# Rotation tables from one scaled base, fold by halves, value sums chosen per period, last exps by query halves and 103 VectorE bursts in a fused state-space and attention kernel

## The chip, the cores and the metric

The kernel runs on one core of a Trainium2 chip. The metric is the device time of one execution in microseconds (us). Most executions of a kernel agree within 0.3%. Engines: PE is TensorE (matmul), PEld its weight loads, DVE is VectorE, ACT is ScalarE, POOL is GpSimd, SP is SyncE.

## The reference, cut to what matters

```python
def reference(A_x, A_Lambda_re, ..., B_x, B_wqkv, B_wo, gate_w):      # cut
    x = A_x                                     # 1 x 2048 x 1024, bf16
    g = _sigmoid((x * gate_w).sum(-1, keepdims=True))
    # A: diagonal complex state space, 1024 states
    Lam_bar = jnp.exp(dt * Lam)
    B_bar = ((Lam_bar - 1.0) / Lam)[:, None] * Bmat
    # h[t] = Lam_bar * h[t-1] + B_bar x[t];   a = 2 Re(C h) + x * Dskip
    # B: attention with 32 heads of 32 channels, softmax over 2048 keys
    p = _softmax(q @ k.T * (Dh ** -0.5)); b = (p @ v) @ wo
    return g * a + (1 - g) * b
```

Two things matter for the argument. The attention needs 32 x 2048 x 2048 exponentials, which is what ScalarE does for nearly the whole time (busy for 904.4 of 920.3 us). The state space is done with "rotation tables" (sines and cosines of multiples of each state's angle, built on VectorE), scans on VectorE, and dense matmuls before and after them.

## The kernel before

The exps are 512 *bursts* of two tiles of 128x1024. Around each burst lies a *period*: PE does the scores of the next burst, some quarters of value sums (exps times V, four 33-column matmuls each) and up to five *dense* 512-column matmuls of projections and state space. Dense matmuls gather in one output bank, which VectorE must *evict* before PE can start the next group (the prediction shows such a wait, 0.40 us at 292.82). In some bursts ("VectorE bursts") ScalarE does half of the first tile less, and four VectorE instructions do it instead.

The order of instructions on every engine is fixed when the kernel is built. A layout program in it carries a clock for PE, ScalarE and VectorE, made of figures written into it, and fills VectorE's gaps by them. The gaps of the first 16 bursts, the *opening*, are filled by `spare`:

```python
    def spare(self, us):
        while self.nmath and us > 0:
            us -= self.bg2[0][0]            # booked cost of the next small instruction
            self.nmath -= 1
            self.bg2.pop(0)[1]()
    # ... in the opening, behind an eviction of Q: self.spare(0.5); of V: self.spare(1.0)

    def fill(self, limit):                  # behind the opening
        while True:
            for src in self.sources():
                c = src[0][0]               # booked cost
                # ... cut
                if c == 0 or self.dve_t + c <= limit:
                    src.pop(0)[1]()
                    self.dve_t += c
                    # ... cut
```

The tables, eight blocks of two products and two sums, with their booked costs:

```python
    def table_ops(self, j):
        # ... lo, lor, hi: two short series, broadcast to 128 x 2 x 32 x 16
        for k, y in ((0, lo), (2, lor)):
            ops.append((1.136, lambda ...: e.tensor_tensor(prod[:, k:k + 2], hi, y, ALU.mult)))
        for r, op in ((0, ALU.subtract), (1, ALU.add)):
            ops.append((0.6, lambda ...: e.tensor_tensor(out, prod[:, 2 * r], prod[:, 2 * r + 1], op)))
```

How many quarters of value sums a period gets is a cap, and the dense matmuls have a quota:

```python
            cap = 5
            if p in DVB or p + 1 in DVB:            # DVB: the VectorE bursts
                cap = 3
            # ... n = min(cap, ready), 6 in a few places
            quota = 3 if p in DVB else 5 if p + 1 in DVB and ... else MM_PER_PERIOD
```

The end, cut: sums of burst 510, four preloading matmuls, sums of 511, one reciprocal, two norms, transposition, checks and flag while PE transposes, outputs, evictions.

```python
        self.pv([(NBURST - 2, q) for q in range(4)])
        preload()
        self.pv([(NBURST - 1, q) for q in range(4)])
        # reciprocal, norm and transposition of both query tiles
        check(63, 64, 63, 65, 2)
        # flag; outputs; evictions; stores
```

## Time and profile before

| | before |
|---|---|
| median of 3 runs | 921.74 us (921.31 to 922.07) |
| span of the profiled run | 920.3 us |
| busy: ScalarE, PE, VectorE | 904.4, 884.9 (from an incomplete record, see the result), 758.0 us |
| start of burst 0; start of burst 72 | 9.82; 142.56 us |
| bursts 72 to 504 (93 VectorE bursts among them) | 754.56 us |
| burst 504 to the end of the last exp | 14.40 us |
| last exp to the end of the span | 8.79 us |

The lines are shown in the prediction. How to read such a kernel: when one engine is busy nearly all the time, "busy" says little. The starts of its 1024 instructions say more. What a burst takes from its start to the next one's above 2 x 0.904 us (or 0.478 + 0.904 for a VectorE burst; the prediction works out these steps) is its *lateness*.

### The profile page before, as it was taken

The numbers are of one execution on the slowest core, as the hardware profiler recorded it, in microseconds if no ns is written. First come the engines' busy times: TensorE is split into PE (matmuls) and PEld (weight loads), VectorE is DVE, ScalarE is ACT, GpSimd is POOL, SyncE is SP. The second block draws the span as 40 slices with busy tenths as digits, with TensorE's granted clock in tenths as the row PEclk, the third lists the DMA queues.
The fourth block names the chain that finished last, engine by engine and source line by source line (L and its number), as shares of the span: only waits on it lengthen the run. The fifth ranks groups of instructions, "written<-read, shape, count | busy, mean of one in ns | idle before, by whom it ended". The sixth has DMA issues, their size and how long they took to land.

```text
span 920.3 us, 33392 instructions
## 1 busy us (share of the span) xinstructions
PE 884.9 (96%) x14969; PEld 516.3 (56%) x15188; DVE 758.0 (82%) x1369; ACT 904.4 (98%) x1034; POOL 6.5 (1%) x31
## 2 busy tenths in 40 slices
PE   8999999999999999999999999999999999999996
PEld 4556655755575555565557555556655655555553
DVE  2799999999989889999889975669999866675665
ACT  6999999999999999999999999999999999999996
POOL 0000000000000000000000000000000000000000
PEclk9999999999999999999999999999999999999998
DMA  9546822213302324112142113123320212524312
GB/s 200 111 82 114 120 48 40 47 42 73 82 9 56 62 59 93 47 36 53 51 82 43 42 46 86 44 63 53 51 64 8 68 60 82 162 78 131 113 63 75
DMA packets 166436, 65.35 MB, mean 71 GB/s; under 512 B 146704, under 2 KB 154896, under 8 KB 166288
## 3 DMA queue, kind: packets, MB, share of 16 engines
q1 hardware_dynamic: 164128, 62.62, 30.6%
q8 instruction: 120, 1.97, 0.9%
q10 hardware_dynamic: 2160, 0.53, 0.3%
q14 instruction: 28, 0.23, 0.1%
HBM read 21.24 MB, written 12.58 MB: 37 GB/s over the span
## 4 chain that ended last, share of the span: by engine, by line
ACT 69%; PE 25%; DVE 2%; SPq 1%; issue 1%; DMA 1%; DVEq 0%
ACT f_pt L1693 59%; PE f_ps L1765 7%; PE f_ps L1677 5%; PE f_ps L1513 4%; PE f_ps L1485 4%; PE f_ps L1453 3%; ACT f_wb L1716 2%; ACT f_OT L1693 2%; ACT f_Et L1693 2%; ACT f_cT_re L1693 2%; ACT f_cT_im L1693 2%; PE f_ps L1473 1%; ACT f_ub L1716 1%; SPq L1080 1%; DMA f_xT<-in_A_x_dram 1%
## 5 line engine op out<-in xcount | busy, mean ns | idle before, releaser
L1693 ACT ACTIVATE f_pt<-f_ps 128x1024 bf16<-128x1024 f32 x848 | 801.8, 1141 | 1.2 <-PE f_ps L1677 1.0
L1765 PEld LDWEIGHTS f_ps<-f_V,f_pt 128*128 128x128 bf16 x6784 | 235.0, 96 | 136.5 <-issue 86.6
L1765 PE MATMUL f_ps<-f_V,f_pt 128*128 128x33 bf16 x6784 | 288.4, 178 | 0.3
L1677 PE MATMUL f_ps<-f_Q,f_K 32*128 32x256 bf16 x4096 | 217.9, 273 | 6.8 <-ACT f_cT_re L1693 1.0
L1677 PEld LDWEIGHTS f_ps<-f_Q,f_K 32*128 32x128 bf16 x4096 | 70.3, 92 | 122.6 <-ACT f_pt L1693 62.3
L1485 PE MATMUL f_ps<-f_xT,f_wb 128*128 128x512 bf16 x449 | 117.5, 377 | 7.2 <-issue 2.4
L1453 PE MATMUL f_ps<-f_xT,f_wb 128*128 128x512 bf16 x406 | 106.6, 378 | 5.0 <-issue 1.0
L1399 DVE TENSOR_TENSOR_SCAN f_ht<-f_pf,f_init,f_ut 128x512 bf16<-128x512 f32 x64 | 81.0, 1274 | 0.0
L1717 DVE TENSOR_SCALAR f_wb<-f_ps 128x512 f32<-128x512 f32 x77 | 52.8, 686 | 27.7 <-PE f_ps L1677 27.2
L1513 PE MATMUL f_ps<-f_cT_im,f_hp 128*128 128x512 bf16 x183 | 69.1, 378 | 3.0 <-DVE f_Ag L1522 0.5
L1540 PE MATMUL f_ps<-f_wb,f_OT 128*128 128x512 bf16 x219 | 58.0, 378 | 2.1 <-DVE f_xT L1546 0.2
L1473 PE MATMUL f_ps<-f_wb,f_xT 128*128 128x128 bf16 x896 | 59.1, 219 | 0.0
L1485 PEld LDWEIGHTS f_ps<-f_xT,f_wb 128*128 128x128 bf16 x512 | 40.2, 96 | 33.4 <-issue 1.2
L1513 PE MATMUL f_ps<-f_cT_re,f_hp 128*128 128x512 bf16 x153 | 57.8, 378 | 0.6
L1716 ACT ACTIVATE f_wb<-f_ps 128x512 bf16<-128x512 f32 x77 | 53.8, 699 | 0.0
L1724 DVE SCALAR_TENSOR_TENSOR f_wb<-f_Ag,f_wb 128x512 int16<-128x512 f32 x77 | 52.7, 684 | 0.7
L1723 DVE SCALAR_TENSOR_TENSOR f_Ag<-f_wb,f_Ag 128x512 f32<-128x512 uint16 x77 | 52.7, 685 | 0.6
L1722 DVE SCALAR_TENSOR_TENSOR f_Ag<-f_wb 128x512 f32<-128x512 uint16 x77 | 52.6, 683 | 0.1
L1453 PEld LDWEIGHTS f_ps<-f_xT,f_wb 128*128 128x128 bf16 x464 | 36.2, 96 | 28.7 <-issue 0.4
L1473 PEld LDWEIGHTS f_ps<-f_wb,f_xT 128*128 128x128 bf16 x896 | 50.5, 97 | 0.2
L1546 DVE SCALAR_TENSOR_TENSOR f_xT<-f_ps,f_gcol,f_hp 128x512 bf16<-128x512 f32 (+1 forms) x28 | 21.0, 751 | 26.6 <-PE f_ps L1540 26.6
L1391 DVE TENSOR_TENSOR f_tq<-f_ht,f_Et 128x1024 bf16<-128x1024 bf16 x64 | 42.5, 685 | 0.3
(143 smaller groups left out, 872.1 us busy)
## 6 DMA issues: line engine op xcount, KB each, us to landing
ag_scratch<-f_Ag SPq DMA_DIRECT2D x32, 256.0 KB, 2.0
f_hp<-ag_scratch SPq DMA_DIRECT2D x32, 256.0 KB, 2.8
f_wb<-in_B_wqkv_dram SPq DMA_DIRECT2D x21, 256.0 KB, 4.1
out_dram<-f_xT SPq DMA_DIRECT2D x16, 256.0 KB, 2.0
f_xa<-in_A_x_dram SPq DMA_DIRECT2D x32, 64.0 KB, 2.0
f_pf<-in_A_x_dram SPq DMA_DIRECT2D x32, 64.0 KB, 2.0
f_wb<-in_B_wo_dram SPq DMA_DIRECT2D x1, 1024.0 KB
f_OT<-f_On SPq DMA_TRANSPOSE x63, 2.3
```

The costliest lines, as they stand in the source:

```text
L1399: ops.append((1.192, lambda ri=ri: dve(lambda e: e.tensor_tensor_scan(ht[:, ri, :], rr, ut[:, ri, :], self.init[:, ri, j:j + 1], ALU.mult, ...
L1453: mms.append((1, lambda e, f, l, a=a: e.matmul(ps[:, bank, :], w[:, g % 2, part, a, :], xT[:, a, 512 * ch:512 * (ch + 1)], start=f, stop=l ...
L1473: m = e.matmul(ps[:, bank, 128 * q:128 * (q + 1)], xT[:, a, 128 * kt:128 * (kt + 1)], w[:, g % 2, 2, a, :], start=(a == 0), stop=(a == 7))
L1485: mms.append((1, lambda e, f, l, a=a: e.matmul(ps[:, 7, :], bT[:, n % 2, ri, a, :], xT[:, a, 512 * ch:512 * (ch + 1)], start=f, stop=l), [ ...
L1513: mms.append((1, lambda e, f, l, j=j, ri=ri: e.matmul(ps[:, 7, :], hp(tq, ri, j), cT[ri][:, j, 512 * cb:512 * (cb + 1)], start=f, stop=l), ...
L1540: mms.append((1, lambda e, f, l, j=j: e.matmul(ps[:, 7, :], OT[:, j, 256 * qb + 128 * r:256 * qb + 128 * (r + 1)], wo[j][0][:, 512 * cb:51 ...
L1677: m = e.matmul(ps[:, 2 * sl[z] + h % 2, 256 * kl:256 * (kl + 1)], K[32 * h:32 * h + 32, g % 2, 128 * kt:128 * (kt + 1)], Q[32 * h:32 * h + ...
L1693: self.act(lambda e: e.activation(self.tile[p], ps[:, 2 * s:2 * s + 2, :], ACT.Exp, bias=OCTAVES * LN2, scale=LN2 / 128), [("S", s)], [("p ...
L1716: self.S.op("act", lambda e: e.activation(t[:, 0, :], ps[:, 2 * s, :], ACT.Exp, bias=OCTAVES * LN2, scale=LN2 / 128), reads=[("S", s)], wr ...
L1717: self.S.op("dve", lambda e: e.tensor_scalar(xi, ps[:, 2 * s + 1, :], BITS_0, BITS_MIN, ALU.add, ALU.max), reads=[("S", s)], writes=[("xi" ...
L1723: (0.603, lambda: self.dve(lambda e: e.scalar_tensor_tensor(xw, lo, CUBE_C, xw, ALU.add, ALU.mult), [I, W], [W], "exp_c")),
L1765: m = e.matmul(ps[:, 6, o:o + 33], self.tile[p][:, h2, 256 * kl + 128 * qt:256 * kl + 128 * (qt + 1)], V[:, g % 2, 2 * i + kl, h, :], star ...
```

## The change

Its intent: free VectorE of table and series work, use that for 7 more VectorE bursts (96 to 103), fit the value sums to what is left of each period, and shorten the end by working on query halves. The diff, cut to its core:

```diff
-DVB_RUNS = ((65, 65), (70, 70), ... (508, 508))           # 96 bursts
+DVB_RUNS = ((67, 67), (70, 70), ... (506, 510))           # 103 bursts; ORDER of dense groups is new as well
+PV_FREE = 72
+SPARE_K = (0.0, 0.0, 0.7, 1.3, 1.3, 2.2, 1.0, 0.8)        # gaps filled behind K's evictions, too
+SPARE_V = (1.0, 0.7, 1.3, 1.3, 1.3, 1.3, 1.3, 1.3)
+PV_MOST = 7
+PV_ROUND = 0.5
@@ series: 232 columns rather than 400; then the base, among the opening's small instructions
+        for n, (u, v) in enumerate(((0, 0), (1, 1), (0, 1), (1, 0))):
+            add(1.14, lambda e, ...: e.tensor_tensor(pr[n]..., hi[u], lo[v], ALU.mult), ...)
+        for r, op in ((0, ALU.subtract), (1, ALU.add)):
+            add(1.14, lambda e, ...: e.tensor_tensor(self.base[:, r], pr[2 * r], pr[2 * r + 1], op), ...)
@@ tables: per block of eight one copy, three scalings, six sums
+            ops.append((0.21, lambda: self.dve(lambda e: e.tensor_scalar(sc(a), base, w(1, a), None, ALU.mult), ...
+            ops.append((0.21, lambda: self.dve(lambda e: e.scalar_tensor_tensor(out(r, a), base[:, r], w(0, a), sc(a)[:, 1 - r], ALU.mult, op), ...
@@ fold: 512 columns at a time, booked 0.35 and 0.62, and begun as each block of C lands
@@ 24 two-column copies from VectorE to GpSimd
@@ value sums from burst 72 on
+        n = int((ta - self.T - QK_PE - dense * MM_PE - 0.1) / PV_PE + PV_ROUND)
+        n = max(min(n, PV_MOST), least, 1)
@@ from burst 508 on, the last outputs ahead of the value sums
+            if p >= REST and cur is None and order and outs and outs[0][1].left == 1 and p >= outs[0][0]:
+                order.pop(0)
+                dn = outs.pop(0)[1]
+                dn.pieces[0][1]()
+                dn.evac()
@@ last burst: two exps, one for each query half, both heads together; the end
+        self.pv([(last - 1, q) for q in range(4)])
+        preload()
+        pv(0)
+        norm(0)
+        pv(1)
+        xp(0)
+        norm(1)
+        out(0)
+        xp(1)
+        out(1)
+        # four evictions with four stores; then check and flag
```

## The prediction

> **What bounds the kernel now.** I read the page's first two parts, then a table of stretches, then the chain of work that ended last, then the timeline of single stalls and of the end.
>
> ```profile
> span 920.3 us, 33392 instructions
> PE 884.9 (96%) x14969; PEld 516.3 (56%) x15188; DVE 758.0 (82%) x1369; ACT 904.4 (98%) x1034; POOL 6.5 (1%) x31
> ACT 69%; PE 25%; DVE 2%; SPq 1%; issue 1%; DMA 1%; DVEq 0%
> L1693 ACT ACTIVATE f_pt<-f_ps 128x1024 bf16<-128x1024 f32 x848 | 801.8, 1141 | 1.2 <-PE f_ps L1677 1.0
> ```
>
> ```profile
> 0.00:9.82 9.82, 7.96 (x53) 3.98 (x54) 0.70 (x2) 1.87 (x3) 1.98 (x13) 1.00 0.95 196
> ...
> 46.00:230.00 184.00, 180.22 (x3187) 107.73 (x3227) 172.56 (x276) 184.00 (x204) 1.98 (x6) 1.00 0.42 71
> 230.00:530.00 300.00, 292.16 (x5046) 171.76 (x5120) 277.54 (x500) 299.45 (x346) 1.48 (x6) 1.00 0.25 55
> 530.00:620.00 90.00, 87.14 (x1432) 47.69 (x1459) 59.92 (x111) 89.89 (x105) 1.04 (x6) 1.00 0.21 61
> ...
> 911.52:920.30 8.78, 1.91 (x14) 0.76 (x15) 3.30 (x19) 1.75 (x5) 0.00 (x0) 0.71 0.28 94
> ```
>
> In the second fence the columns after the stretch are its length and the busy time of PE, PEld, DVE, ACT and POOL, then clock, DMA share and GB/s. ScalarE, which does the softmax exponentials, is busy in every microsecond from 46 to 911.5. VectorE has 4 to 7% free from 46 to 530 and a third free after. So the span has three parts: 9.82 us until the first exp, 901.7 us of exps (to 911.5), and 8.8 us of end.
>
> The exps are 512 bursts of two tiles, 128x1024 each. In 96 bursts (the 77 and 19 instructions of line 1716) VectorE computes half of the first tile with four instructions and ScalarE does only 512 columns. "Busy" hides waiting here, as records of neighbouring exps overlap. I therefore took the step from one start to the next from the trace's single records: 904 ns after a full tile where nothing is late (its fastest value and the median of all 928), 478 ns after a half one. 928 x 0.904 + 96 x 0.478 = 884.8 us is what the stream needs; it takes 901.7. The difference, 16.9 us, is lateness of the matmuls that feed it, with 0.6 us of it for a few small other activations.
>
> What makes them late I read by counting matmuls in each burst's period. A period of two full exps is 1.81 us. PE's parts, from starts on the timeline: scores 0.34 us, each quarter of a burst's value sum (four 33-column matmuls) 0.10, each 512-column matmul 0.216, about 0.1 for order. Thirty periods hold five quarters and five 512-column matmuls: 0.34+0.50+1.08+0.1 = 2.02 us. They are late by 0.14 us on average, 4.1 us together. One of them:
>
> ```profile
> 644.32 4.08 ACT L1693 ACTIVATE f_pt<-f_ps 128x1024 bf16<-128x1024 f32 x4
> ...
> 645.20 0.47 PE L1765 MATMUL f_ps<-f_V,f_pt 128*128 128x33 bf16 x12
> ...
> 645.52 1.24 PE L1485 MATMUL f_ps<-f_xT,f_wb 128*128 128x512 bf16 x5
> ...
> 646.59 0.36 PE L1765 MATMUL f_ps<-f_V,f_pt 128*128 128x33 bf16 x8
> ...
> 646.88 0.40 PE L1677 MATMUL f_ps<-f_Q,f_K 32*128 32x256 bf16 x8
> ```
>
> The scores at 644.76 and those at 646.88 are 2.12 us apart with PE hardly pausing: too much was put there. The other kind has PE idle behind a VectorE eviction of its only output bank:
>
> ```profile
> 292.01 0.75 DVE L1522 SCALAR_TENSOR_TENSOR f_Ag<-f_ps,f_gcol,f_Ag 128x512 f32<-128x512 f32 x1
> ...
> 292.82 1.04 PE L1485 MATMUL f_ps<-f_xT,f_wb 128*128 128x512 bf16 x4 [0.40 <-DVE f_Ag L1522]
> ...
> 294.23 1.94 ACT L1693 ACTIVATE f_pt<-f_ps 128x1024 bf16<-128x1024 f32 x2 [0.20 <-PE f_ps L1677]
> ```
>
> Split over all bursts: periods whose parts sum to more than the exps have 7.1 us of lateness (6.4 after burst 72), the others 9.1, of which some 3 us are steps of 16 ns[...].
>
> [...]
>
> **The change part by part.**
>
> 1. VectorE bursts 96 to 103. I expanded both lists: 7 more, five of them in bursts 64 to 127, two fewer in 160 to 223, the rest late. Each takes 0.904-0.478 = 0.426 us from ScalarE, the engine that sets the stream: 7 x 0.426 = -3.0 us.
>
> 2. What VectorE pays. Seven bursts, four instructions of 0.685: +19.2. Angle series at 232 instead of 400 columns:[...] -4.2. Tables before: 16 x 1.215 + 16 x 0.685 = 30.4. After: six products and sums for the base at 1.215 = 7.3, then per block of eight one copy, three 256-column scalings and six 128-column sums. From the rows, a 256-column fp32 one with a column scalar is 0.48, its fixed part 0.21, so 128 columns about 0.345[...]; ten of these x 8 = 27. In all 34, +4, though each is issued before the last has quite ended. Fold by halves pays its fixed part twice: about +3.6. Copies to GpSimd: 24 x 0.161 = -3.9. Sum about +19 of records, 758 to some 777 us, 85% of the new span. So VectorE doesn't become the bound, but 93% in the dense stretch makes evictions no earlier. I charge +0.8 us for that.
>
> 3. Value sums chosen per period. From burst 72 the number of quarters is what still fits before the exps end (rounded to nearest, at most 7), not a cap of 3, 5 or 6. With five 512-column matmuls planned, 1.81-0.34-1.08-0.1 leaves room for about three quarters, not five. PE's mean need is 805/512 = 1.57 us a burst (scores 174, sums 207, the rest 424) against 1.72 from ScalarE, so there is room elsewhere. Of the 6.4 us of overload lateness I expect two thirds back: -4.0 (an estimate from the counts above, the least certain term).
>
> 4. Opening: order and slots are nearly unchanged; a 0.63 us stall at 44 us sits behind small parameter instructions, which now are spread over the opening: -0.3.
>
> 5. The end. Before:
>
> ```profile
> 911.98 0.21 DVE L2060 RECIPROCAL f_rc<-f_ps 128x8 f32<-128x8 f32 x1
> ...
> 912.91 0.55 ACT L2069 ACTIVATE f_OT<-f_ps 128x128 bf16<-128x128 f32 x2 [1.39 <-PE f_ps L2066]
> ...
> 914.05 1.27 DVE L2091 SCALAR_TENSOR_TENSOR f_xT<-f_ps,f_Et 128x512 bf16<-128x512 f32 x2
> ```
>
> From the last exp's end (911.52) to the last eviction (915.32) is 3.8 us. After, the first query half's sum, norm, transposition and output run under the second half's exp. What follows it is one chain: sums 0.4, reciprocal 0.25, norm 0.4, transposition and copy 0.6, output 0.6, eviction 0.75 = 3.0. So -0.8. The checks and the flag go behind the evictions (about 1.3 us), but the stores take longer (issue at 915.39, landed at 919.81), so 5 us from last eviction to end stay.
>
> Sum: 921.74 - 3.0 + 0.8 - 4.0 - 0.3 - 0.8 = 914.4 us.
>
> **The rivals.** (a) Overload only moves: quarters put off must be taken before their buffers are needed, and every new VectorE burst makes a period of 1.38 us that holds scores, three quarters and three 512-column matmuls (1.29) with nothing over. Then term 3 is -1 and the time 917.5. For it: PE already is at 96%. Against: that figure counts overlapping records, and the sum of parts is 91%. (b) VectorE becomes what PE waits for: the added bursts lie where it has 4 to 7% free. Then lateness behind evictions grows by 3 to 4 us and the time is near 918. Against: series and copies leave, and the list takes bursts out of 160 to 223. (c) The reordering also removes most of the eviction waits (6 us beyond the 16 ns steps): 911. (d) The end is set by flag[...] instead of the stores: term 5 vanishes, 915.2, or +1 more if the flag's 1.3 us isn't hidden.
>
> **Range and chances.** The first term is firm; term 3 could be -1 to -7, the end +0.5 to -2, VectorE 0 to +3. That gives 911.0 to 918.5 for eight in ten. 2% is 18.4 us. Removing every stall would give 16 us and with the seven tiles nearly 20, so faster by 2% is near impossible: 1%. Slower by 2% would need a broken schedule: 1%. Within 2%: 98%.
>
> **What would show it.** Right: 103 half activations (about 0.48 us a step) and 921 full ones; ScalarE's busy time near 897 and still whole from 46 us to the last exp; VectorE 770 to 780; total lateness near 13 us instead of 17, with periods of five quarters and five 512-column matmuls almost gone; last exp to last eviction about 3.0 us. Wrong: lateness unchanged or moved to periods waiting for evictions; PE waits on VectorE growing between 115 and 230 us; the last eviction later than 3.5 us after the last exp because the VectorE burst at 510 still occupies VectorE; or an end longer than 8.8 us.

In fp32 a two-operand series instruction takes 567 ns at 400 columns before and 393 at 232 after (0.174 us less), a `tensor_scalar` 368 and 280 (0.088 less), and a scaling takes 346. The fold's +3.6 was too low: its 1024-column instructions of 1279 and 745 ns became two of some 742 and two of 478 each, 32.4 us before and 39.1 after. The 24 copies took 0.161 us each on VectorE and 0.55 on average on GpSimd (0.19 to 0.71; GpSimd's spans are rough). The steps of 16 ns can be counted in the trace: 129 exps start 920 or 921 ns after the one before rather than 904, and 21 start 494 or 495 ns after it rather than 478 (130 and 35 in the changed kernel); that no schedule would remove them is not shown.

## The result, and the profile after

| | before | after |
|---|---|---|
| median | 921.9 us (4 runs) | 936.02 us (935.87 to 936.66, 4 runs) |
| ratio after / before | | 1.0153, 95% interval 1.0135 to 1.0170 |
| span of the profiled run | 920.3 | 934.8 us |
| start of burst 72 | 142.56 | 150.36 (+7.8) |
| bursts 72 to 504 | 754.56 | 755.40 (+0.8, with 6 more VectorE bursts in it; see the spread below) |
| burst 504 to the end of the last exp | 14.40 | 16.22 (+1.8) |
| last exp to the end | 8.79 | 12.84 (+4.05) |
| lateness before burst 72; bursts 72 to 504 | 3.4; 13.1 | 10.9; 16.5 |

A ratio is the mean time of one kernel's fast runs over that of the other's fast runs of the same rounds, so not quite the ratio of the medians. The kernel's output is correct. It is 14 us slower, where 7 us faster was forecast, and lies above the predicted range. The four stretches add up to the 14.5 us between the spans.

The page of the changed kernel: span, busy times, the engines of the chain of work that ended last, and the group of the full exps.

```profile
span 934.8 us, 33765 instructions
...
PE 905.0 (97%) x15188; PEld 513.6 (55%) x15188; DVE 774.6 (83%) x1461; ACT 904.2 (97%) x1033; POOL 20.0 (2%) x58
...
PE 80%; DVE 14%; ACT 3%; DMA 2%; issue 1%; SPq 0%; DVEq 0%
...
L1778 ACT ACTIVATE f_pt<-f_ps 128x1024 bf16<-128x1024 f32 x839 | 798.5, 1135 | 5.6 <-PE f_ps L1755 4.5
```

VectorE's 774.6 us is close to what the prediction said (777). ScalarE's busy time did not fall at all, although 7 bursts were taken from it: the records of neighbouring exps overlap by some 0.23 us (1.135 us long, 0.904 apart), so a short lateness shrinks the overlap and does not show as idle time (in the changed kernel a full exp that starts 1.0 to 1.1 us after the one before is 1.046 us long on average, one on time 1.141).

The third line invites a false reading. Before, the chain ran over ScalarE for 69% and over PE for 25%; now it seems to have moved to PE. But the trace of the kernel before holds only 14969 of its 15188 matmuls (the 219 that are missing are all dense 512-column ones; the weight loads are complete), and so do those of e1 to e4, e13, e14 and e15, within one record. Two complete traces, of the kernel before with 20 fewer VectorE bursts (e8) and of a run as fast as the kernel before (e11), show the chain on PE as well:

```profile
PE 69%; ACT 27%; DVE 3%; issue 0%; DVEq 0%
...
PE 85%; DVE 6%; ACT 4%; SPq 2%; DMA 2%; issue 1%; DVEq 0%
```

So PE's share tells nothing, nor does its busy time (884.9 against 905.0). What is left is VectorE's share: 2 to 3% in the kernel before and in e8, 14% now, and 5 to 6% in the runs whose table pieces are cut (e1, e3, e11).

**The opening.** The timeline of the changed kernel around burst 9 (start, duration, engine, instruction, then in brackets the idle time before it and what ended it):

```profile
26.67 0.61 PE L1173 MATMUL f_ps<-f_xT,f_wb 128*128 128x256 bf16 x4
...
26.87 2.35 DVE L1314 TENSOR_TENSOR f_hp<-f_OT 128x1024 f32<-128x1024 f32 x2
...
29.14 0.42 DVE L1185 CAST f_K<-f_ps 128x256 bf16<-128x256 f32 x1
...
29.61 0.40 PE L1755 MATMUL f_ps<-f_Q,f_K 32*128 32x256 bf16 x8 [1.87 <-DVE f_K L1185]
...
30.04 1.02 ACT L1778 ACTIVATE f_cT_re<-f_ps 128x1024 bf16<-128x1024 f32 x1 [1.25 <-PE f_ps L1755]
```

Two products of the new base (L1314, 2.35 us) stand on VectorE ahead of the eviction of K, whose matmuls (L1173) ended at 27.28; PE waits 1.87 us for it and ScalarE then 1.25 us for PE. With a second such place at burst 12 this makes burst 16 start 2.4 us late.

**Bursts 16 to 72.** The same timeline around burst 30:

```profile
67.18 1.02 PE L1520 MATMUL f_ps<-f_xT,f_wb 128*128 128x512 bf16 x4
...
67.77 1.12 DVE L1399 SCALAR_TENSOR_TENSOR f_Et<-f_OT 128x128 bf16<-128x128 f32 x3
...
68.93 0.62 DVE L1394 TENSOR_SCALAR f_OT<-f_OT 128x256 f32<-128x256 f32 x2
...
69.46 0.29 DVE L1403 CAST f_Et<-f_OT 128x256 bf16<-128x256 f32 x1
69.66 0.68 DVE L1526 CAST f_ub<-f_ps 128x512 bf16<-128x512 f32 x1
...
70.40 1.04 PE L1488 MATMUL f_ps<-f_xT,f_wb 128*128 128x512 bf16 x4 [1.08 <-DVE f_ub L1526]
...
71.81 1.94 ACT L1778 ACTIVATE f_pt<-f_ps 128x1024 bf16<-128x1024 f32 x2 [1.07 <-PE f_ps L1755]
```

The dense group (L1520) ends at 68.20, but its eviction to `f_ub` starts only at 69.66, as VectorE has been running pieces of a table one after the other since 66.14; the last three (two scalings and a copy) are in the lines. Then PE may go on, and ScalarE gets its scores 1.07 us late. Such places, of 0.3 to 1.3 us each, lie at bursts 22, 24, 32, 34, 50, 56 and 66. The groups of the table's pieces (count, then busy us, mean ns of one):

```profile
L1399 DVE SCALAR_TENSOR_TENSOR f_Et<-f_OT 128x128 bf16<-128x128 f32 x48 | 16.7, 348 | 1.1
...
L1394 DVE TENSOR_SCALAR f_OT<-f_OT 128x256 f32<-128x256 f32 x24 | 7.8, 346 | 0.1
...
L1403 DVE CAST f_Et<-f_OT 128x256 bf16<-128x256 f32 x8 | 2.3, 286 | 0.0
```

The layout program books each of the 80 at 0.21 us, so 16.8 us for what takes 26.8. It believes that VectorE is done with them when it isn't, and sets them ahead of an eviction that will then be late.

**The last bursts and the end.** From the timeline after (the corresponding lines of before are in the prediction's section on the end):

```profile
913.08 0.38 PE L1575 MATMUL f_ps<-f_wb,f_OT 128*128 128x512 bf16 x1 [0.41 <-DMA f_OT<-f_On]
...
916.77 0.39 PE L1575 MATMUL f_ps<-f_wb,f_OT 128*128 128x512 bf16 x1 [0.66 <-DVE f_xT L1581]
...
920.05 1.94 ACT L1763 ACTIVATE f_pt<-f_ps 128x1024 bf16<-128x1024 f32 x2 [0.82 <-PE f_ps L1755]
...
920.83 0.69 DVE L1809 SCALAR_TENSOR_TENSOR f_ub<-f_ut 128x512 int16<-128x512 f32 x1
...
921.58 0.29 PE L1850 MATMUL f_ps<-f_V,f_ub 128*128 128x33 bf16 x4 [0.89 <-DVE f_ub L1809]
...
921.94 1.87 PE L2155 MATMUL f_ps<-f_Et,f_ident 128*128 128x512 bf16 x4
...
923.60 0.43 PE L2166 MATMUL f_ps<-f_V,f_pt 128*128 128x33 bf16 x8
...
929.96 0.15 DVE L2224 CAST flag<-f_ps 1x1 int32<-1x1 f32 x1 [0.26 <-PE f_ps L2222]
```

Read it in steps. The last outputs (L1575), now ahead of the value sums, wait for the transposed last-but-one unit and then for each other's eviction; behind them the scores come late, and both exps of the last burst start 0.82 us late. VectorE's own part of burst 510 ends at 921.52, so its sums (L1850) start at 921.58, when the first query half, whose exp ended at 921.08, has been ready for half a microsecond. Then come four preloading matmuls (L2155), and only at 923.60 the sums of the first half (L2166), 1.6 us after *both* halves were done: nothing of the first half's work lies under the second half's exp. The flag is computed behind the evictions. Moreover the clock had halved:

```profile
922.00:934.80 12.80, 4.87 (x31) 1.66 (x27) 3.87 (x17) 1.15 (x3) 0.00 (x0) 0.50 0.13 45
```

In this stretch (columns as in the prediction's table of stretches) the granted clock is 0.50; the records show it halving at 919.21, before the last exps, and the four preloading matmuls take 1.87 us. In the mended run below they take 1.02. What halves the clock, these runs don't show: PE was busy for 1.83 of the 3.41 us before 919.21.

### The profile page after: what moved, and what is told of

Same layout as the page of the kernel before. It is cut to its first block, busy times and chain, and to the rows that moved or that the text cites. A ratio compares the mean times of both kernels' runs of the same rounds, so it can differ in the third digit from the quotient of the medians.

```text
span 934.8 us, 33765 instructions
## 1 busy us (share of the span) xinstructions
PE 905.0 (97%) x15188; PEld 513.6 (55%) x15188; DVE 774.6 (83%) x1461; ACT 904.2 (97%) x1033; POOL 20.0 (2%) x58
## 4 chain that ended last, share of the span: by engine, by line
PE 80%; DVE 14%; ACT 3%; DMA 2%; issue 1%; SPq 0%; DVEq 0%
PE f_ps L1850 22%; PE f_ps L1755 15%; PE f_ps L1548 11%; PE f_ps L1520 10%; PE f_ps L1488 9%; PE f_ps L1575 5%; PE f_ps L1508 5%; DVE f_tq L1426 2%; ACT f_pt L1778 1%; DVE f_ht L1434 1%; DVE f_Et L1399 1%; DVE f_ub L1526 1%; DVE f_ut L1426 1%; DVE f_Q L1493 1%; DMA f_xT<-in_A_x_dram 1%
## 5 line engine op out<-in xcount | busy, mean ns | idle before, releaser
L1850 PEld LDWEIGHTS f_ps<-f_V,f_pt 128*128 128x128 bf16 x6712 | 233.4, 96 | 139.3 <-issue 86.1
L1850 PE MATMUL f_ps<-f_V,f_pt 128*128 128x33 bf16 x6712 | 285.9, 178 | 2.3 <-DVE f_On L1864 2.0
L1755 PE MATMUL f_ps<-f_Q,f_K 32*128 32x256 bf16 x4096 | 211.1, 273 | 4.1 <-DVE f_K L1185 2.3
L1520 PE MATMUL f_ps<-f_xT,f_wb 128*128 128x512 bf16 x512 | 131.0, 377 | 2.7 <-DVE f_Ag L1557 1.1
L1755 PEld LDWEIGHTS f_ps<-f_Q,f_K 32*128 32x128 bf16 x4096 | 65.6, 92 | 120.5 <-ACT f_pt L1778 65.5
L1488 PE MATMUL f_ps<-f_xT,f_wb 128*128 128x512 bf16 x464 | 119.2, 379 | 3.4 <-DVE f_Q L1493 1.8
L1802 DVE TENSOR_SCALAR f_wb<-f_ps 128x512 f32<-128x512 f32 x83 | 57.1, 687 | 36.7 <-PE f_ps L1755 35.3
L1548 PE MATMUL f_ps<-f_cT_re,f_hp 128*128 128x512 bf16 x192 | 72.7, 378 | 0.4 <-DVE f_Q L1493 0.2
L1575 PE MATMUL f_ps<-f_wb,f_OT 128*128 128x512 bf16 x252 | 65.5, 378 | 1.9 <-DVE f_xT L1581 1.2
L1801 ACT ACTIVATE f_wb<-f_ps 128x512 bf16<-128x512 f32 x83 | 59.6, 718 | 0.4 <-PE f_ps L1755 0.4
L1520 PEld LDWEIGHTS f_ps<-f_xT,f_wb 128*128 128x128 bf16 x512 | 40.3, 96 | 35.3 <-issue 3.0
L1809 DVE SCALAR_TENSOR_TENSOR f_wb<-f_Ag,f_wb 128x512 int16<-128x512 f32 x83 | 56.8, 684 | 0.6
L1807 DVE SCALAR_TENSOR_TENSOR f_Ag<-f_wb 128x512 f32<-128x512 uint16 x83 | 56.7, 683 | 0.2
L1526 DVE CAST f_ub<-f_ps 128x512 bf16<-128x512 f32 x48 | 33.1, 690 | 13.5 <-PE f_ps L1520 13.1
```

Of the source, the lines that this page charges most:

```text
L1488: mms.append((1, lambda e, f, l, a=a: e.matmul(ps[:, bank, :], w[:, g % 2, part, a, :], xT[:, a, 512 * ch:512 * (ch + 1)], start=f, stop=l ...
L1520: mms.append((1, lambda e, f, l, a=a: e.matmul(ps[:, 7, :], bT[:, n % 2, ri, a, :], xT[:, a, 512 * ch:512 * (ch + 1)], start=f, stop=l), [ ...
L1548: mms.append((1, lambda e, f, l, j=j, ri=ri: e.matmul(ps[:, 7, :], hp(tq, ri, j), cT[ri][:, j, 512 * cb:512 * (cb + 1)], start=f, stop=l), ...
L1575: mms.append((1, lambda e, f, l, j=j: e.matmul(ps[:, 7, :], OT[:, j, 256 * qb + 128 * r:256 * qb + 128 * (r + 1)], wo[j][0][:, 512 * cb:51 ...
L1755: m = e.matmul(ps[:, 2 * sl[z] + h % 2, 256 * kl:256 * (kl + 1)], K[32 * h:32 * h + 32, g % 2, 128 * kt:128 * (kt + 1)], Q[32 * h:32 * h + ...
L1801: self.S.op("act", lambda e: e.activation(t[:, 0, :], ps[:, 2 * s, :], ACT.Exp, bias=OCTAVES * LN2, scale=LN2 / 128), reads=[("S", s)], wr ...
```

## The experiments

"Burst 72" is the start of burst 72 in the profiled run, "middle" the time from there to burst 504, "end" the time from the last exp's end to the span's end. Differences of time in the text are made from ratios times 922 us, as these use runs of the same rounds. The profiled starts have a spread of their own: burst 72 lies between 149.9 and 151.1 us in the eight runs that have the changed kernel's opening, and the middle between 754.3 and 755.4 in the eight that have its middle (after, e1 to e6, e11; mean 754.8). Small differences are therefore read from means of several runs, or not at all. Part of that spread goes with the clock: in e5, e6, e7, e15 and e16 it was halved for 3.41 us near 30 us, behind the stall of burst 9, and burst 16 starts at 41.8 to 42.6 us there, against 41.4 to 41.9 in the other runs with the full base in the opening's gaps. The 95% interval of a ratio is 1.2 to 2.5 us to either side. A difference between two runs of less than some 2.3 us is therefore not shown by the times alone; where I rely on one, it is for what the starts in the traces show beside it.

| run | median us | ratio to before | burst 72 | middle | end |
|---|---|---|---|---|---|
| before | 921.9 to 922.4 | 1 | 142.56 | 754.56 | 8.79 |
| after | 936.02 | 1.0153 | 150.36 | 755.40 | 12.84 |
| e1_short_tables | 929.30 | 1.0083 | 144.00 | 754.51 | 12.38 |
| e2_short_base | 933.54 | 1.0126 | 147.99 | 754.66 | 13.20 |
| e3_short_both | 927.63 | 1.0072 | 141.82 | 754.75 | 13.05 |
| e4_rest | 934.42 | 1.0135 | 150.08 | 755.24 | 13.09 |
| e5_rest_no510 | 931.51 | 1.0100 | 150.68 | 754.82 | 10.03 |
| e6_end_mended | 929.19 | 1.0081 | 150.41 | 754.27 | 8.38 |
| e7_after_20_fewer | 943.59 | 1.0229 | 151.10 | 761.07 | 13.60 |
| e8_before_20_fewer | 929.32 | 1.0077 | 142.17 | 762.25 | 8.70 |
| e9_91_picked | 941.33 | 1.0208 | 150.31 | 758.20 | 13.55 |
| e10_91_capped | 939.04 | 1.0188 | 149.92 | 757.88 | 12.98 |
| e11_all_cuts | 922.32 | 1.0002 | 142.62 | 754.54 | 8.36 |
| e12_mended | 930.01 | 1.0084 | 149.64 | 755.15 | 8.51 |
| e13_before_new_end | 923.99 | 1.0011 | 142.63 | 754.98 | 10.71 |
| e14_before_mended_end | 922.68 | 0.9997 | 142.89 | 754.86 | 8.77 |
| e15_after_no_436_444 | 938.06 | 1.0164 | 151.14 | 756.06 | 13.06 |
| e16_old_lists | 930.24 | 1.0085 | 150.93 | 755.53 | 8.89 |
| e17_right_booking | 924.43 | 1.0027 | 143.58 | 755.51 | 8.37 |
| e18_booking_and_base | 923.13 | 1.0009 | 142.90 | 755.35 | 8.72 |

My theory after reading the two traces: (i) the table pieces and the base, set ahead of evictions, lose the first 72 bursts; (ii) the end loses by its own order; (iii) in the middle the choice per period gains nothing. The rival to (i) and (iii) was a VectorE or PE that is simply too full.

### Cutting the tables' work

e1: same instructions in the same order, each table piece on an eighth of its columns (wrong result).

```diff
-e.tensor_scalar(sc(a), base, w(1, a), None, ALU.mult)
+e.tensor_scalar(sc(a)[:, :, 0:1], base[:, :, 0:1], w(1, a), None, ALU.mult)      # sums and copy likewise
```

> The changed kernel with every VectorE instruction in its place, but the 80 pieces of the rotation tables (scaling, sum, copy) cut to an eighth of their columns, so that each costs about its fixed part; the result is wrong on purpose. Theory A (the pieces take 0.29 to 0.35 us where the program that lays out the order books 0.21, so evictions come late behind them in the first 72 bursts): the stalls near 69 and 120 us vanish, burst 72 starts 4 to 5 us earlier than in the changed kernel, and the time falls by as much, 936 to 931-932. Rival B (VectorE is too full over its whole length, the table pieces are only a part of the load): less than 1.5 us. Rival C (lateness only moves to the next eviction): burst 72 earlier by less than 2 us.

Measured: 929.3 us, 6.5 less; burst 72 at 144.00, 6.4 earlier. That is theory A, and more than it expected. The pieces' groups in this run:

```profile
L1399 DVE SCALAR_TENSOR_TENSOR f_Et<-f_OT 128x16 bf16<-128x16 f32 x48 | 11.1, 231 | 1.1
...
L1394 DVE TENSOR_SCALAR f_OT<-f_OT 128x32 f32<-128x32 f32 x24 | 5.0, 232 | 0.1
```

So an eighth of the columns still takes 231 ns of the 348: about two thirds of such a piece is its fixed part. Only 9.2 us of VectorE's records went (48 x 0.117 + 24 x 0.114 + 8 x 0.112), and 6.5 us of them reached the time. The eviction of burst 30, 1.46 us late above, is 0.18 us late here (its dense group ends at 66.53):

```profile
65.51 1.02 PE L1520 MATMUL f_ps<-f_xT,f_wb 128*128 128x512 bf16 x4
...
66.71 0.69 DVE L1526 CAST f_ub<-f_ps 128x512 bf16<-128x512 f32 x1
```

e2: the same for the base.

```diff
-e.tensor_tensor(pr[n]..., hi[u], lo[v], ALU.mult)                        # 1024 columns
+e.tensor_tensor(pr[n]...[:, 0:1], hi[u][:, 0:1], lo[v][:, 0:1], ALU.mult)   # 128 columns; base zeroed first
```

> The changed kernel with the four products and two sums of the base table cut from 1024 to 128 columns, in the same places of the same order (base filled with zeros first; wrong on purpose). Theory A (the base's 1.2 us instructions, set between the evictions of the opening, hold up bursts 9 and 12): burst 16 starts 2 to 2.5 us earlier, the stalls at 29.6 to 30 us vanish, the time falls by 2 to 2.5 us to about 933.7. Rival (those stalls have another cause, such as the loads of the opening): nothing before burst 16, under 0.5 us in all.

Measured: 933.5 us, 2.5 less. Burst 16 starts at 39.32 (39.50 before, 41.86 after). Theory A, with its number.

e3: both cuts.

> Both cuts together (wrong on purpose). If the two causes lie in different bursts and add up, burst 72 starts within 1 us of where it starts in the kernel before (it started 7.8 us later in the changed one), and the time is 928 to 930. If they hide each other, or if later slack eats the gain, 931 or more.

Measured: 927.6 us, 7.5 less; burst 72 at 141.82, 0.7 us ahead of the kernel before. The two causes lie in different bursts and add up in the starts (8.5 us, against 6.4 and 2.4 alone). In the times they add up less well, 7.5 of 9.0, within the intervals; one of e3's four runs took 931.56 us and the others 927.1 to 927.7. No third cause is needed to explain the loss before burst 72; the cuts leave VectorE less work than it had before the change, so a small one could hide.

### The end

e4: the last outputs behind the value sums again.

```diff
-            if p >= REST and cur is None and order and outs and outs[0][1].left == 1 and p >= outs[0][0]:
+            if False:
```

> The changed kernel with one line back: from burst 508 on, the last output matmuls are taken behind the value sums of their burst, as before the change, not ahead of them. The result stays right. Theory (ahead of the sums, they wait for the transposed last-but-one unit and for each other's eviction and hold up the scores of 508 to 511[...]): the 2.3 us between bursts 508 and 511 shrink to under 1, the time falls by 2 to 4 us to 932 to 934. Rival (the matmuls only wait elsewhere, in the tail, where they then lie on the path to the end): bursts 508 to 511 improve but the time from the last exp to the end grows by as much, the time within 1 us of 936.

Measured: 934.4 us, 1.7 less. Burst 504 to the last exp shrinks from 16.22 to 13.95 us, by the full 2.3. But the end stays at 13.1 us, so the gain is a little less than expected: the end has a cause of its own.

e5: burst 510 given back to ScalarE as well.

```diff
-... (482, 498), (501, 501), (506, 510))
+... (482, 498), (501, 501), (506, 506))
```

> The changed kernel with the last outputs behind the value sums again (as in the run before) and burst 510 taken from VectorE's list and left whole to ScalarE, 102 VectorE bursts. Right result. With burst 510 on VectorE, its four instructions ended 0.5 us after the last exp, and the sums of 510 and all of the end waited for them. Theory (that chain sets the end): ScalarE's stream gets 0.4 us longer, but the stretch from the last exp to the last eviction falls from 7.0 to about 5 us[...], so the time falls by 1 to 2 us against the run before, 934.4 to about 933. Rival (the order of PE's own work, the preloading ahead of the first half's sums, sets it): unchanged within 0.6 us.

Measured: 931.5 us, 3.2 less than e4, twice what was expected. Last exp to last eviction fell from 6.98 to 3.79 us, the end from 13.1 to 10.0. One VectorE burst so near the end costs 3 us net (ScalarE's stream is 0.43 us longer without it, the end 3.06 shorter).

e6: the order of the end mended too.

```diff
+        preload()
         self.pv([(last - 1, q) for q in range(4)])
-        preload()
@@
         out(0)
+        # check (VectorE), then the flag's matmul behind xp(1)
         xp(1)
         out(1)
-        evac(0, 0, "dve")
+        evac(0, 0, "act")
```

> The same, with two more changes of order in the end: the preloading of two output banks set ahead of the last sums of burst 510 rather than between these and the first half's sums, and the last check and the flag computed while PE transposes instead of behind the evictions (one eviction goes to ScalarE for it). Right result. Theory (term 5 of the prediction fails only by the order, not by the idea): last exp to last eviction about 3.5 us, the flag no longer last, the end after the last exp 8.5 to 9.5 us instead of 13, the time 929 to 931. Rival (the splitting by query halves costs in itself, in waits for semaphores and small instructions): still over 11 us after the last exp, the time above 932.5.

Measured: 929.2 us, 1.8 less than e5 and 6.6 less than the changed kernel; the end takes 8.38 us, as expected and 0.4 less than before the change. Last exp to last eviction takes 4.3 us, though, not 3.5 (before: 3.8). Its timeline says why the halves gain nothing (the last exp ends at 919.07):

```profile
918.59 0.35 PE L2166 MATMUL f_ps<-f_V,f_pt 128*128 128x33 bf16 x8
918.99 0.18 DVE L2173 RECIPROCAL f_rc<-f_ps 128x4 f32<-128x4 f32 x1 [0.91 <-PE f_ps L2166]
...
919.71 0.35 PE L2166 MATMUL f_ps<-f_V,f_pt 128*128 128x33 bf16 x8 [0.76 <-DVE f_On L2174]
...
921.98 0.13 DVE L2222 CAST flag<-f_ps 1x1 int32<-1x1 f32 x1
```

Both halves add up in one bank. VectorE's norm of the first half reads it, so the second half's sums, whose exps are ready at 919.07, start at 919.71. The first half is early by less than what the second then waits: 0.48 us against 0.64. This is read from the trace; no run with two banks was made. The clock, halved at 921.40 here, seems a small part: in e14 and e18, where it is halved only within or behind the last output matmuls, the same stretch takes 4.14 us, 0.15 less.

e13 and e14 put the changed and the mended end on the kernel before, whose last VectorE burst is 508 and whose outputs are in their old place.

```diff
-        sl = [(2 * self.p) % 3, (2 * self.p + 1) % 3]
+        sl = [(2 * self.p + 2) % 3, (2 * self.p + 3) % 3]
+        # last exps by query halves, check from burst 501, the new tail: as changed (e13), as mended (e14)
```

> The kernel before with the changed end alone (last exps by query halves, four separate stores, checks begun at burst 501, check and flag behind the evictions); its 96 VectorE bursts, last of them 508, and the place of its last outputs are kept. Right result. The prediction's term 5 has 0.8 us gained: 921.1. Theory (the end lost 6.8 us in the changed kernel mostly by meeting VectorE's burst 510 and the outputs set ahead of the sums; the preloading between the sums and the flag behind the evictions cost some 2.3): 0 to 2.5 us slower, 922 to 924.5.

> The kernel before with the mended end alone (preloading ahead of the last sums, check and flag while PE transposes). Right result; it could beat both kernels. In the mended run the stretch from the last exp to the end was 8.4 us against 8.8 before: 0.4 us faster, 921.5. The prediction's term 5: 0.8 us faster. Rival (the flag[...] set the end whatever the order): no gain, 922.

Measured: e13 1.0 us slower by ratio (interval -0.3 to +2.2), its end 10.71 us against 8.79; e14 0.3 us faster (interval -1.5 to +1.0), its end 8.77. So the end as changed costs 1.9 us by itself in the trace and 1.0 in the times, whose interval includes zero; the rest of its loss came from meeting burst 510 and the outputs set ahead. In e13's profiled run the clock was halved from 910.26 to 913.68, over the preloading ahead of the first half's sums, which took 1.87 us there; how much of the 1.9 is the clock, these runs don't part. Mended it gains nothing, as the rival of e14 had it; the reason that the rival gives is not shown.

### What a VectorE burst is worth

e7 and e8: 20 VectorE bursts between 208 and 436 given back to ScalarE, in the changed kernel and in the kernel before.

```diff
-DVB = {B for lo, hi in DVB_RUNS for B in range(lo, hi + 1, 4)}
+DVB = {... } - {237, 245, 254, 261, ... 402, 417}      # e7; e8: - {209, 214, 222, 230, ... 421, 430}
```

> The changed kernel with 20 of the 54 VectorE bursts between 208 and 436 given back to ScalarE (83 left). Right result. Each moves 0.426 us to ScalarE. Theory 1 (term 1 of the prediction: ScalarE sets the stream, a VectorE burst saves its full 0.426): 8.5 us slower, 944.5. Theory 2 (in the changed kernel PE sets the stretch, the saved time comes back as lateness of the scores): 3 to 6 us slower, 939 to 942, and the sum of lateness falls by 2.5 to 5.5 us.

> The kernel before with 20 of its 52 VectorE bursts of the same stretch given back to ScalarE (76 left), all else planned as it was. Right result. Theory 1: 8.5 us slower, 930.4. Theory 2 for this kernel, whose PE is ahead more often: 6 to 8 us slower. If both kernels lose the same, the density of VectorE bursts is no reason for the missing gain of the middle; if the changed one loses less, it is.

Measured: 7.0 us slower for the changed kernel (1.0229 - 1.0153), 7.1 for the kernel before: 0.35 us a burst in both, 83% of the 0.426, but with some 0.1 either way from the intervals, so the full 0.426 is not excluded. By this the density of bursts is no reason. The profiled middle is less even: +5.7 us after (its lateness falls by 2.9, which theory 2 had asked for), +7.7 before. The rest of e7's time lies outside the bursts that its edit takes, and these stretches differ from run to run. So a burst saves 0.28 us (the profiled middle) to 0.35 (the times) in the changed kernel; which, these runs don't settle.

### Value sums per period

The changed lists can't be built with the old caps: the layout program runs into buffers that aren't free. With 12 bursts fewer and dense groups allowed to overtake each other they can. e9 is the control with those 91 bursts, e10 differs from it in one line.

```diff
-PV_FREE = 72
+PV_FREE = 440        # e10: old caps for bursts 72 to 439
```

> The control for the next run. The changed kernel with 91 VectorE bursts (91, 86, 172, 294, 299, 302, 307, 310, 315, 378, 436 and 444 given back to ScalarE, without which the next run's schedule can't be built) and with the groups of dense matmuls free to overtake each other where the next in the list isn't ready. Value sums still chosen per period from burst 72. Right result. From the two runs with 20 bursts fewer a burst is worth 0.36 to 0.38 us, so 12 fewer make 936.0 some 4.5 us longer: about 940.5.

> The same 91 bursts and freedom of order, but value sums by the old fixed caps from burst 72 to 439, chosen per period only from 440 on. Right result. Theory P (the prediction's term 3: choosing per period takes away overload, worth 4.0 us): 3 to 4 us slower than the control. Theory F (the choice fills periods up to the brim by its own rounded figures, so overload only becomes thinner and spreads over more periods; rival (a) of the prediction): within 1 us of the control, or faster by up to 2 us.

Measured: the control 941.3 us, as expected; the capped one 939.0, 1.8 us *faster* by ratio, which is within the intervals. Its middle is 0.3 us shorter, most of the difference lies outside, so I read from it no more than this: choosing per period gained nothing, and theory P's 3 to 4 us are excluded. That is theory F.

What became of the overload I counted from the weight loads, as the matmul records of the kernel before are incomplete (the prediction's thirty periods with 4.1 us, and its 6.4 us of overload, are counted from these). In the kernel before 39 periods held five quarters and five dense matmuls, with 5.1 us of lateness; in the changed one a single period does. Five and four are in 172 periods with 4.5 us before and in 180 with 6.2 after. New are 42 VectorE periods of four or five quarters and three dense ones, with 3.8 us. Periods whose parts exceed their exps, from burst 72 on, are 178 in both kernels, with 9.0 us of lateness before and 12.5 after. In e9 they are 156 with 10.7, in e10 165 with 10.4. The overload was not taken away; it moved, and costs more where it now lies.

### Are these all the causes?

e11: both cuts (wrong) and the mended end; no new edit.

> The changed kernel with both cuts of the tables (wrong result on purpose) and the mended end (102 VectorE bursts). If the opening's VectorE work (8.4 us when both cuts ran alone) and the end (6.8 us in the mended run) are separate causes, the time is 936.0 - 8.4 - 6.8 = 920.8, between 920 and 922; the kernel before has 922. If they overlap, or if something else sets the end then, 923 or more.

Measured: 922.3 us, ratio 1.0002. Opening and end account for all of the loss against the kernel before. They don't account for the gain that five or six more VectorE bursts should have brought (see the sum below).

e12: a right result, with the base left to the ordinary filling. It has the mended end and, to be buildable, 100 VectorE bursts and dense groups that may overtake each other; the cut shows the base alone.

```diff
-                self.nmath = len(self.bg2)
+                self.nmath = self.n_before_base      # spare() stops ahead of the base
```

> A mended version with the right result: the base table's products are no longer set between the evictions of the opening but behind it, by the planner's ordinary filling; the end mended as before; dense groups may overtake each other; 100 VectorE bursts, as four around 190 and the one at 510 don't fit and two others do. The table pieces keep their too low booking. Theory: against the mended-end run's 929.2, the base's 2.5 us come back in part (its 7.3 us of VectorE now lie in the first bursts), and 2 bursts fewer cost 0.8: 927 to 929. Rival (the base holds up evictions wherever it is put): 930 or more.

Measured: 930.0 us: the rival. Burst 16 starts as before (39.49), but burst 72 at 149.64. What was won by burst 16 was lost again by burst 72. That the base's 7.3 us, moved behind the opening, pushed the still underbooked pieces into worse places is the likely reading; this run alone doesn't show it. It fits e18 below, where the same move with true bookings keeps its gain.

e15: the changed kernel without VectorE bursts 436 and 444. In its middle there is one knot that the kernel before doesn't have:

```profile
784.10 0.48 DVE L1356 SCALAR_TENSOR_TENSOR f_Ag<-f_xa,f_gcol,f_drow 128x256 f32<-128x256 bf16 x1 [1.43 <-DMA ag_scratch<-f_Ag]
...
785.62 0.47 PE L1850 MATMUL f_ps<-f_V,f_pt 128*128 128x33 bf16 x12 [1.12 <-DVE f_On L1864]
```

These are timeline lines of the changed kernel: VectorE stands 1.43 us behind the store of its scratch, the normalization comes late behind that, and PE with it. Bursts 432 to 448 take 29.24 us against 27.65 before.

```diff
+DVB -= {436, 444}        # in the kernel: the list without them
```

> The changed kernel without VectorE bursts 436 and 444 (101 left). Right result. Theory (these two hit the place where VectorE stands behind the store of its scratch and delay PE by 1.15 and 0.47 us at bursts 435 and 444): burst 448 starts 0.5 to 0.9 us earlier although ScalarE has 0.85 us more to do, the time 935 to 935.5. Rival (a general fullness: the lateness moves to the next bursts): 0.4 to 0.8 us slower, 936.4 to 936.8.

Measured: 938.1 us, 1.0 us slower by ratio: a miss, though within the intervals. Bursts 432 to 448 took 29.00 us, 0.24 less although they hold 0.85 us more for ScalarE, so the knot is looser, but the time doesn't show it, and other stretches of this run were longer by more than that. (The 29.24 us of the changed kernel's profile are the longest of the eight runs with its middle; their mean is 28.77.)

### Booked cost or true cost

That the pieces' duration matters was shown by e1; that the *booking* is at fault was still argued. With the lists of before (order of dense groups, 96 bursts), caps throughout and the mended end, the changed code can be built with either booking.

```diff
# e16
-ORDER, DVB_RUNS as changed; PV_FREE = 72
+ORDER, DVB_RUNS as before;  PV_FREE = 600
# e17, on top
-            ops.append((0.21, ... e.tensor_scalar(sc(a)
+            ops.append((0.31, ... e.tensor_scalar(sc(a)
-            ops.append((0.21, ... e.scalar_tensor_tensor(out(r, a)
+            ops.append((0.36, ... e.scalar_tensor_tensor(out(r, a)
-            ops.append((0.21, ... e.tensor_copy(Et
+            ops.append((0.29, ... e.tensor_copy(Et
# e18, on top: e12's edit
```

> The changed code with the lists of before (order of dense groups, the 96 VectorE bursts), fixed caps for the value sums throughout, and the mended end. New tables as changed: booked at 0.21 us a piece, the base set into the opening's gaps; fold by halves. Right result. Theory A (the new tables' placing and booking lose the opening, whatever the lists): burst 72 starts 6 to 8 us later than before, the time 928 to 930. Rival (the new order of the dense groups is what loses it): burst 72 within 3 us of before, the time under 925.5. For the middle: if the lists and the choice per period cause its lateness, bursts 72 to 504 take 754.6 us as before, within 0.5; if the tables and the fold do, 756 or more.

> The same, with three figures changed in the program that lays out the order: a scaling booked at 0.31, a sum at 0.36, a copy at 0.29 us, near what their records show, instead of 0.21. Same instructions, same sizes, right result. Theory A (booking is the cause): evictions are then set ahead of the pieces, 4 to 6.5 us come back by burst 72, the time falls as much, to about 924. Rival (VectorE simply has 27 us more to do there): less than 2 us.

> The same as the run before, and the base table's products and sums taken out of the opening's gaps and left to the ordinary filling, with their right figures. Right result; all mends together, with 96 VectorE bursts. Theory A: the 2.4 us at bursts 9 and 12 come back too, 921.5 to 922.5, level with the kernel before; nothing in it is left that should be faster by more than 0.5 us. Rival (as in the mended run above, the base costs as much where it goes instead): no change, 924.

Measured: e16 930.2 us, burst 72 at 150.93, 8.4 us late under the old lists: the new order of the dense groups is not the cause. e17 924.4 us: three figures of the layout program took 5.4 us off by ratio, and burst 72 starts 7.4 us earlier (e16's profiled run was the slowest of its five, 931.5 us, with a halved clock for 3.41 us near 30 and again near 136 us). VectorE's busy time is 758.4 us in one and 758.9 in the other: not a bit of its work went. The timeline of e17 around burst 30 shows the order that follows from true figures:

```profile
66.35 0.69 DVE L1496 CAST f_K<-f_ps 128x512 bf16<-128x512 f32 x1
...
66.95 0.28 DVE L1403 CAST f_Et<-f_OT 128x256 bf16<-128x256 f32 x1
...
67.27 1.13 DVE L1399 SCALAR_TENSOR_TENSOR f_Et<-f_OT 128x128 bf16<-128x128 f32 x3
67.28 1.02 PE L1488 MATMUL f_ps<-f_xT,f_wb 128*128 128x512 bf16 x4
```

The eviction (L1496) runs first, the pieces behind it, and PE's next dense group carries no bracket: it waits for nothing. e18: 923.1 us, 1.7 less than e17 by ratio, ratio 1.0009 (0.9996 to 1.0023). It is the best version of the changed code with a right result, and it does not beat the kernel before. Nor does e14. None of these runs does.

The middle takes 755.53, 755.51 and 755.35 us in e16 to e18, with the old lists and caps, mean 755.5. In before, e13 and e14 the mean is 754.8. So new tables, fold and copies cost some 0.7 us there, between my two expectations.

## Why the prediction was wrong, by its own steps

**Term 1, -3.0 us (7 more VectorE bursts): too large for one of them.** The count and the half tiles are right. A burst is worth 0.35 us by e7 and e8's times, so 7 make -2.5, and by the profiled middle of e7 -2.0; the -3.0 itself lies within the intervals. But one of the 7, burst 510, cost about 3 us where it lay (e5). The prediction named this risk in its last part ("because the VectorE burst at 510 still occupies VectorE"), and then gave it no place in the sum.

**Term 2, +0.8 us (VectorE pays): the step that failed.** Its working of VectorE's *amount* was good: 777 us told, 774.6 found. But it charged an amount, and what counts is where a piece lies. 0.8 stands against 7 to 8 us: e3 takes 7.5 off by cutting table pieces and base, e17 5.4 off by no cut at all. The argument was that VectorE at 85% "doesn't become the bound, but ... makes evictions no earlier". It made them later, wherever 0.35 us pieces were booked at 0.21. The prediction had both numbers: it worked out "about 0.345" for a piece, and the diff says 0.21. It never held them against each other. (That a scaling of 256 columns costs as much as a sum of 128 was its estimate; the traces bear it out, 346 and 348 ns in the changed kernel. From 232 ns at 32 columns in e1 and 346 at 256, a column of an fp32 `tensor_scalar` costs 0.51 ns; from 566 ns at 400 and 1215 at 1024 in the kernel before, one of an fp32 `tensor_tensor` 1.04. And VectorE was not a third free all the way after 530 us: from 620 to 736 it was busy for 107.5 of 116.)

**Term 3, -4.0 us (value sums per period): about zero.** e10 against e9, in the version with 91 VectorE bursts that could be built. The periods of five and five are gone, as told (the thirty were 39, counted in full); rival (a), "overload only moves", is what happened to their lateness. The rounding to nearest and a limit of 7 fill periods to their brim by the layout program's figures.

**Term 4, -0.3 us (opening): the wrong sign.** It said that order and slots are nearly unchanged. The order of PE's work is, but six 1.2 us instructions had joined the list that fills those slots, and a slot of 1.3 us takes two of them if the first leaves 0.16 us over. Nor were the slots unchanged: behind an eviction of V they were 1.0 us before, which by the code one product would have used up. The six in these places are +2.5 us (e2).

**Term 5, -0.8 us (the end): +4 in the end and +1.8 ahead of it.** It counted the chain behind the last exp and missed what stands before it in each engine's order: VectorE's burst 510, the outputs set ahead of the value sums, the preloading ahead of the first half's sums, and the flag behind the evictions. Rival (d), an end set by the flag, fits the end as changed: there the flag is copied at 929.96, behind the last eviction (928.93), and from the end of GpSimd's branch after it to GpSimd's next instruction it is 3.73 us, against 2.83 in the kernel before. (In the nine runs where the flag came before the last eviction this took 2.3 to 3.1 us, in the eleven where it came behind it 3.3 to 4.3; what fills that time is not shown.) And by the trace of e6 the overlap of halves is lost to one bank; even the mended end is only level (e14).

The sum with these in place: 921.9 - 2.5 (term 1) + 7.5 (tables and base, e3) + 6.6 (end and last bursts, e6) = 933.5, and 2.5 us are missing to 936. The middle has most of them: its mean of 754.8 us is the same in both kernels, though six VectorE bursts more should make it 2.1 shorter (at 0.35). New tables, fold and copies are 0.7 of that (e16 to e18). The stretch 432 to 448 is 1.1, as the mean of the same eight runs; e15 loosened it without a gain in time, so its part is read from the trace and not shown by a run. The rest is within the spread. How much of it is the lists and how much the choice per period stays open.

The chances were wrong in kind, not only in size: nearly all weight was put on a gain because each term was taken as an amount of work, and an amount can only lose a little. The range's upper end, 918.5, let VectorE cost at most 3 us more.

## What to carry to other kernels

When the order of instructions is fixed beforehand from booked costs, a change is first to be read for its bookings: hold each booked figure against the record of the same shape, multiply by the count, and look at which waiting engine stands behind the pieces. Cutting an instruction into many small ones changes more than its sum, as two thirds of a 128-column piece is its fixed part (231 of 348 ns are left at an eighth of the columns, e1). And near the end of a kernel a transfer of work to another engine saves its own length at most, while its last instruction delays everything that is left (0.43 us against about 3 for burst 510). Before two traces are compared by counts, busy times or chains of an engine, its records are to be counted in both: 219 missing matmuls made one kernel look bound by another engine.
